# The product with w1 in seven products of quarters for the groups of 256 tokens, and transposed attention weights in two parts a pair

## The chip, the cores and the metric

The kernel runs on one core of one Trainium2 chip. The metric is the device time of a launch in microseconds: 1701.26 us before, the median of three runs (1700.86 to 1701.98). The core has TensorE for products (with a separate count of its weight loads), VectorE (DVE), ScalarE (ACT) and GpSimd (POOL) for elementwise work, and SyncE, which issues transfers.

## The reference

Attention over 8 batches of 8 heads, 576 tokens and 64 values a head, in which only the scores within tau of their row's maximum count; then, per batch, a Fourier mix of the [576, 512] result and a feed-forward pair of products. All is fp32.

```python
scores = scale * q @ k^T                          # [8, 8, 576, 576]
scores = where(scores >= max(scores) - tau, scores, -1e9)
attn   = softmax(scores) @ v                      # -> x [8, 576, 512]
u  = x + real(fft(fft(x, axis=1), axis=2))
un = (u - mean(u)) / sqrt(var(u) + 1e-6)
out = u + maximum(un @ w_ch1, 0) @ w_ch2          # w_ch1 [512, 2048], w_ch2 [2048, 512]
```

## The kernel before

The mean is taken out of w1 once and the variance's factor is applied at the end, so that the feed-forward part works on u, held transposed as u_t in a ring of two batches (1152 tokens). The first 512 tokens go in two groups by plain products; the other 4096 go in 16 groups of 256. For those the second product (with w2) is already done in seven products of quarters by Winograd's form of Strassen's method: both operands are cut into 2 x 2 quarters, sums of quarters are formed, and seven quarter products replace eight. Groups alternate between two orders ("up" and "down"), so that each leaves the sums of the weights as the next one needs them.

Everything TensorE does stands in an order fixed by the program. In each attention step i the scores of one block of 128 queries are made, `softmax` runs on VectorE and ScalarE, and the weights of the step before are transposed (`weights_in_parts`). Between these come three slots, `fill()`, in which the Fourier mix and the feed-forward groups advance by one piece or more: each `yield` ends a piece. From the third batch on, only TensorE's order is fixed; the order on the other engines is a scheduler's. All products share four PSUM banks (tag "mm"), except the scores.

The transposed weights, kept for a pair of heads, and the product with v:

```python
    def weights_in_parts(i):

        n, t = divmod(i, NT)
        e, rec = steps.pop(i)
        if t == 0:


            e_t = sb.tile([128, 8, S], FP32, tag="e_t", bufs=1, name="e_t")
            ends = sb.tile([128, S], FP32, tag="ends", bufs=1, name="ends")
            recs = None
            if rec is not None:
                recs = sb.tile([128, S], FP32, tag="sums", bufs=1, name="recs")
            vt = heads[n][2]
            # ... (v with its columns reversed, for odd pairs)
            heads[n] = (*heads[n][0:2], vt, e_t, ends, recs)
        e_t, ends, recs = heads[n][3:6]
        pe = ps.tile([128, 4, 128], FP32, tag="mm", bufs=4, name="pe")
        nc.tensor.transpose(pe[:, 0, :], e[:, 512:640], ident[:, :])
        kept = [ends]
        if rec is not None:
            nc.tensor.transpose(pe[:, 1, :], rec[:, :], ident[:, :])
            kept.append(recs)
        # ... copies of pe into ends (and recs) by ScalarE; qs: the columns of block t
        for j in range(2 if t < 4 else 1):
            pw = ps.tile([128, 4, 128], FP32, tag="mm", bufs=4, name="pw")
            if j == 1:
                yield
            for c in range(4):
                c0 = (S + D) * j + 128 * c
                nc.tensor.transpose(pw[:, c, :], e[:, c0 : c0 + 128], ident[:, :])
            if t < 4:
                nc.scalar.copy(e_t[:, 4 * j : 4 * j + 4, qs], pw[:, :, :])
            # ... the last block has both heads in one copy

    def weighted_values(n):

        b, p = n // NPAIR, PAIRS[n % NPAIR]
        _, _, vt, e_t, ends, recs = heads.pop(n)
        if n % NPAIR == 0:
            xs[b] = [None] * NPAIR
        x = sb.tile([128, S], FP32, tag=f"x{p}", bufs=1, name=f"x{p}")
        for h in range(2):
            cols = slice(HALF * h, HALF * (h + 1))
            pv = ps.tile([128, 512], FP32, tag="mm", bufs=4, name="pv")
            for c in range(5):
                for j in range(2):
                    nc.tensor.matmul(
                        pv[64 * j : 64 * j + 64, 0:HALF], vt[:, 2 * c + j, :],
                        e_t[:, 4 * j + c, cols] if c < 4 else ends[:, cols],
                        start=(c == 0), stop=(c == 4), skip_group_check=True,
                    )
            if normalized(n):
                nc.scalar.copy(x[:, cols], pv[:, 0:HALF])
            else:
                nc.vector.tensor_tensor(
                    out=x[:, cols], in0=pv[:, 0:HALF], in1=recs[:, cols], op=ALU.mult
                )
        # ... two rows swapped by transfers, for odd pairs
        xs[b][p] = x
```

The rows of a group, the product with w1, and a group of 256 tokens:

```python
    class Rows:


        def __init__(self, g):
            # ... first token, number of 128-row tiles, buffers
        def load(self):
            t = len(self.us)
            c0 = (self.first + 128 * t) % RING
            pn = ps.tile([128, 512], FP32, tag="mm", bufs=4, name="pn")
            for c in range(ND):
                nc.tensor.transpose(
                    pn[:, 128 * c : 128 * (c + 1)], u_t[:, c, c0 : c0 + 128], ident[:, :]
                )
            u = sb.tile([128, DM], FP32, tag="u", bufs=3, name="u")
            for c in (0, 256):
                nc.scalar.copy(u[:, c : c + 129], pn[:, c : c + 129])
                nc.scalar.copy(u[:, c + 129 : c + 256], _reversed(pn[:, c + 129 : c + 256]))
            # ... mean and variance of the row (VectorE)
            self.us.append(u)

        # ... factors(): rstd = 1 / sqrt(var + eps) of the loaded rows (ScalarE, VectorE)
        def add(self, t, cols, product):

            u = self.us[t][:, cols]
            nc.vector.scalar_tensor_tensor(
                out=u, in0=product, scalar=self.rstd[:, t : t + 1], in1=u,
                op0=ALU.mult, op1=ALU.add,
            )

        # ... store(t): the tile of u goes out

    def hidden(g, count, j, ht):

        # ... n tokens from column c0 of the ring; two parts where they straddle its end
        for a, z, at in parts:
            for c in range(ND):
                nc.tensor.matmul(
                    ph[:, a:z], w1[c][:, 128 * j : 128 * (j + 1)], u_t[:, c, at : at + z - a],
                    start=(c == 0), stop=(c == ND - 1), skip_group_check=len(parts) > 1,
                )
        if count % 2 == 0:
            nc.scalar.activation(out=ht, in_=ph[:, 0:n], func=ACT.Relu)
        else:
            nc.vector.tensor_relu(ht, ph[:, 0:n])

    # ... channels(g): the first two groups, by plain products

    def channels_in_quarters(g):
        if g == FIRST:
            first_sums()
        up = (g - FIRST) % 2 == 0
        rows = Rows(g)
        h = [hs[:, BT * j : BT * (j + 1)] for j in range(NJ)]
        a = [
            [[h[NK * k + p][:, 128 * i : 128 * (i + 1)] for p in range(NK)] for k in range(2)]
            for i in range(2)
        ]
        s_tile = sb.tile([128, NK, 128], FP32, tag="sums", bufs=1, name="s_tile")
        s_sum = [s_tile[:, p, :] for p in range(NK)]
        pool = nc.gpsimd

        for count in range(NJ):
            p, k = divmod(count, 2)
            hidden(g, count, NK * k + p, h[NK * k + p])
            if k == 1:

                pool.tensor_tensor(out=s_sum[p], in0=a[1][0][p], in1=a[1][1][p], op=ALU.add)
                if not up:
                    pool.tensor_tensor(out=s_sum[p], in0=s_sum[p], in1=a[0][0][p], op=ALU.subtract)
                pool.tensor_tensor(
                    out=a[1][0][p], in0=a[0][0][p], in1=a[1][0][p], op=ALU.subtract
                )
            yield 4 * ND * BT
            if count in (3, 7):
                rows.load()
                yield ND * 128
            if count == 11:
                rows.factors()

        def product(bank, left, right, start):
            for p in range(NK):
                nc.tensor.matmul(
                    bank[:, 0 : DM // 2], left[p], right[p],
                    start=start and p == 0, stop=p == NK - 1, skip_group_check=True,
                )
                if p % 2 == 1 and p < NK - 1:
                    yield 4 * DM

        # alone(): such a product in a bank of its own, then rows.add() by VectorE
        # ... fifth or seventh; product 1 opens the bank sum_; 2 alone; product 6 adds into sum_, two rows.add();
        # 3 alone; product 4 adds into sum_, rows.add(); seventh or fifth; the sums between them on GpSimd
        # (s_sum, a[0][1]) and VectorE (t_sum)
```

The slots, and the last six batches:

```python
    def fill():
        nonlocal budget, spent
        budget += per_slot
        if mixes:
            mix(1)
        while work and spent < budget and work[0][0] < mixed:
            done = next(work[0][1], None)
            if done is None:
                work.pop(0)
            else:
                spent += done

    # ... the first two batches, every engine's order fixed

    # ...
    for i in range(2 * per_batch, total + 1):
        if i < total:
            scores(i)
            softmax(i)

        n, t = divmod(i, NT)
        nothing = iter(())
        prep = prep_in_parts(n + 1) if t == 3 and n + 1 < B * NPAIR else nothing
        weights = weights_in_parts(i - 1)
        next(prep, None)
        fill()
        next(weights, None)
        fill()
        next(weights, None)
        next(prep, None)
        fill()
        next(prep, None)
        if t == 0:
            weighted_values(n - 1)
            for _ in fold_rows(n - 1):
                pass
            if n + 1 < B * NPAIR:
                load_v(n + 1)
        if i % per_batch == 0:
            start_batch(i // per_batch - 1)
    per_slot = cost(0) / 40
    while mixes or work:
        fill()
```

Of the kernel before, what the change touches and what calls it, by code (L numbers as in the profile page):

```python
# [47 lines left out]
def kernel(  # L48
# [12 lines left out]
    nc = tc.nc  # L61
# [213 lines left out]

    shift = const.tile([128, 1], FP32, name="shift")
# [231 lines left out]
    def weights_in_parts(i):  # L508
# [3 lines left out]
        if t == 0:  # L512


            e_t = sb.tile([128, 8, S], FP32, tag="e_t", bufs=1, name="e_t")
            ends = sb.tile([128, S], FP32, tag="ends", bufs=1, name="ends")
            recs = None
            if rec is not None:
                recs = sb.tile([128, S], FP32, tag="sums", bufs=1, name="recs")
            vt = heads[n][2]  # L520
            if PAIRS[n % NPAIR] % 2:
# [11 lines left out]
        e_t, ends, recs = heads[n][3:6]  # L533
        pe = ps.tile([128, 4, 128], FP32, tag="mm", bufs=4, name="pe")
# [5 lines left out]
        for c, dst in enumerate(kept):  # L540
            if t < 4:
                nc.scalar.copy(dst[:, 128 * t : 128 * t + 128], pe[:, c, :])
            else:
                for j in range(2):
                    hp = slice(64 * j, 64 * j + 64)
                    nc.scalar.copy(dst[hp, 512:S], pe[hp, c, hp])
        qs = slice(128 * t, min(128 * t + 128, S))
# [15 lines left out]
    def weighted_values(n):  # L563

        b, p = n // NPAIR, PAIRS[n % NPAIR]
        _, _, vt, e_t, ends, recs = heads.pop(n)
        if n % NPAIR == 0:
            xs[b] = [None] * NPAIR
        x = sb.tile([128, S], FP32, tag=f"x{p}", bufs=1, name=f"x{p}")
        for h in range(2):  # L570
            cols = slice(HALF * h, HALF * (h + 1))
            pv = ps.tile([128, 512], FP32, tag="mm", bufs=4, name="pv")
            for c in range(5):
                for j in range(2):
                    nc.tensor.matmul(  # L575
                        pv[64 * j : 64 * j + 64, 0:HALF], vt[:, 2 * c + j, :],
                        e_t[:, 4 * j + c, cols] if c < 4 else ends[:, cols],
                        start=(c == 0), stop=(c == 4), skip_group_check=True,
                    )
            if normalized(n):  # L580
                nc.scalar.copy(x[:, cols], pv[:, 0:HALF])  # L581
            else:
                nc.vector.tensor_tensor(
                    out=x[:, cols], in0=pv[:, 0:HALF], in1=recs[:, cols], op=ALU.mult
                )
# [254 lines left out]

# [400 lines left out]
```

## Time and profile before

| what | value |
|---|---|
| median of three runs | 1701.26 us |
| profiled execution | 1704.2 us from first to last instruction |
| mean TensorE clock granted | 0.995 of full speed |
| hidden product, line 805 | 2560 matmul records, 543.1 us busy |
| quarter products with w2, line 899 | 1792 records in three rows, 426.2 us busy |
| product with v, line 575 | 1280 records |
| transposes of the weights, line 554 | 1152 records, 168.9 us busy |

An instruction of TensorE has two records in the profile where it is an fp32 product, and one where it is a transpose. The busy time of a row is the time covered by its records together; as matmuls overlap in the pipeline, the mean of one record is longer than the distance between two. Where a rate is wanted, the distance from start to start in a timeline is the thing to read. A row of the profile names the line, the engine, the operation, what it writes and reads, the shape and the count; then busy us and the mean ns of one; then the idle time of its engine just before it, and what ended that idle time. GpSimd's spans are rough.

### The profile page before, as it was taken

To read this page: it belongs to the slowest core of one execution; us is meant where nothing else is said; L and a number is where in the kernel's file an instruction comes from. 1 tells how busy PE (TensorE), PEld (TensorE's weight loads), DVE (VectorE), ACT (ScalarE), POOL (GpSimd) and SP (SyncE) were. 2 spreads that over 40 slices of the span, in tenths; PEclk is the share of its full clock that TensorE was granted. 3 is DMA by queue.
4 is the path that set the end of the run, shared out by engine and by line. 5 is a ranking of instruction groups with operands and counts; after the bars stand their busy time and mean duration, and the time that the engine had idled before them with its cause. 6 is when DMAs were issued, how large, how long until landed. Compare 5 with 4: busy or idle time off the path is not lost.

```text
span 1704.2 us, 26612 instructions
## 1 busy us (share of the span) xinstructions
PE 1659.1 (97%) x9558; PEld 1266.5 (74%) x9558; DVE 1051.0 (62%) x2593; ACT 689.7 (40%) x1620; POOL 604.3 (35%) x1075
## 2 busy tenths in 40 slices
PE   8988989999999999999999999999999999999998
PEld 4555555576787787778878777777777788788887
DVE  6886885665566666656545766666565766543233
ACT  5764765343444343434333434343434444311100
POOL 5664563031312442243331233314341424242333
PEclk9999999999999999999999999999999999999999
DMA  5323222100010101000010010101011010000000
GB/s 163 110 53 108 71 71 55 30 19 21 22 34 22 30 6 41 22 27 22 13 28 27 22 33 11 34 22 28 21 29 34 15 35 2 13 1 13 13 13 13
DMA packets 130377, 57.34 MB, mean 34 GB/s; under 512 B 121123, under 2 KB 121125, under 8 KB 130246
## 3 DMA queue, kind: packets, MB, share of 16 engines
q1 hardware_dynamic: 128854, 55.35, 12.0%
q8 instruction: 76, 1.25, 0.3%
q14 instruction: 55, 0.45, 0.1%
q10 hardware_dynamic: 1392, 0.30, 0.1%
HBM read 46.02 MB, written 9.44 MB: 33 GB/s over the span
## 4 chain that ended last, share of the span: by engine, by line
PE 87%; DVE 5%; ACT 5%; DMA 1%; issue 1%; SPq 0%; POOL 0%; ACTq 0%; DVEq 0%; POOLq 0%
PE ph L805 28%; PE po L899 23%; PE pv L575 9%; PE sc L431 8%; PE pw L554 6%; PE po L829 3%; PE sc L442 2%; ACT e L467 2%; DVE e L475 2%; PE py L674 1%; PE pa L691 1%; DVE neg L459 1%; PE pa L695 1%; PE pe L535 1%; PE pn L765 1%; PE pq L396 1%
## 5 line engine op out<-in xcount | busy, mean ns | idle before, releaser
L805 PE MATMUL ph<-u_t,w 128*128 128x256 f32 (+2 forms) x2560 | 543.1, 362 | 5.8 <-ACT y_e L684 4.1
L805 PEld LDWEIGHTS ph<-u_t,w 128*128 128x128 f32 x2560 | 428.6, 191 | 75.4 <-issue 12.0
L459 DVE TENSOR_REDUCE neg<-sc 128x1 f32<-128x576 f32 x288 | 205.9, 751 | 217.3 <-PE sc L431 202.2
L467 ACT ACTIVATE e<-sc,neg 128x576 f32<-128x576 f32 x288 | 211.5, 734 | 309.8 <-DVE neg L459 309.6
L884 POOL TENSOR_TENSOR s_tile<-hs 128x128 f32<-128x128 f32 x128 | 62.1, 485 | 638.0 <-DVE hs L812 536.4
L475 DVE SCALAR_TENSOR_TENSOR e<-sc,thr,e 128x576 f32<-128x576 f32 x288 | 227.2, 814 | 61.1 <-ACT thr L471 60.0
L899 PE MATMUL po<-w,hs 128*128 128x256 f32 x1024 | 242.8, 382 | 0.0
L899 PEld LDWEIGHTS po<-w,hs 128*128 128x128 f32 x1024 | 187.3, 190 | 29.6 <-issue 7.0
L556 ACT COPY e_t<-pw 128x512 f32<-128x512 f32 x256 | 148.3, 593 | 119.5 <-PE pw L554 119.0
L554 PE MATMUL pw<-ident,e 128*128 128x128 f32 x1152 | 168.9, 273 | 11.1 <-ACT kT L404 4.8
L431 PE MATMUL sc<-kT,qT 64*128 64x288 f32 x1024 | 165.9, 430 | 7.8 <-DVE e L475 7.3
L554 PEld LDWEIGHTS pw<-ident,e 128*128 128x128 f32 x1152 | 135.8, 141 | 34.8 <-ACT kT L404 5.6
L812 DVE TENSOR_SCALAR hs<-ph 128x256 f32<-128x256 f32 (+2 forms) x144 | 60.5, 420 | 149.1 <-PE ph L805 134.6
L431 PEld LDWEIGHTS sc<-kT,qT 64*128 64x128 f32 x1024 | 92.0, 186 | 68.4 <-issue 43.1
L810 ACT ACTIVATE hs<-ph 128x256 f32<-128x256 f32 (+2 forms) x144 | 55.1, 383 | 214.7 <-PE ph L805 206.4
L787 DVE SCALAR_TENSOR_TENSOR u<-po,rstd,u 128x256 f32<-128x256 f32 (+1 forms) x164 | 76.1, 482 | 84.1 <-PE po L899 84.0
L491 DVE TENSOR_SCALAR e<-e,den 128x576 f32<-128x576 f32 x216 | 123.5, 608 | 3.0
L899 PE MATMUL po<-hs,s_tile 128*128 128x256 f32 x512 | 122.4, 383 | 0.0
L899 PEld LDWEIGHTS po<-hs,s_tile 128*128 128x128 f32 x512 | 93.9, 190 | 16.2 <-issue 3.0
L857 POOL TENSOR_TENSOR hs<-hs,s_tile 128x128 f32<-128x128 f32 x128 | 60.4, 490 | 83.2 <-PE po L899 82.7
L857 POOL TENSOR_TENSOR s_tile<-s_tile,hs 128x128 f32<-128x128 f32 x128 | 70.7, 579 | 28.2 <-PE po L899 28.2
L581 ACT COPY x<-pv 128x288 f32<-128x288 f32 x48 | 19.2, 399 | 147.9 <-PE pv L575 142.7
(169 smaller groups left out, 2208.3 us busy)
## 6 DMA issues: line engine op xcount, KB each, us to landing
hs<-in_moe_w_ch_dram SPq DMA_DIRECT2D x23, 512.0 KB, 4.2
out_dram<-u SPq DMA_DIRECT2D x36, 256.0 KB, 2.2
qk_in<-in_q_dram SPq DMA_DIRECT2D x64, 128.0 KB, 2.3
v_in<-in_v_dram SPq DMA_DIRECT2D x64, 128.0 KB, 2.4
qk_in<-in_k_dram SPq DMA_DIRECT2D x31, 128.0 KB, 2.5
w<-in_moe_w_ch_dram SPq DMA_DIRECT2D x6, 512.0 KB, 7.8
qk_in<-in_k_dram SPq DMA_DIRECT2D x31, 64.0 KB, 2.3
stage<-in_moe_w_ch_dram SPq DMA_DIRECT2D x3, 512.0 KB, 4.3
```

Source lines behind the costliest of these rows:

```text
L431: nc.tensor.matmul(sc[j][:, c, 0:HALF], qT[hp, 128 * t : 128 * t + 128], kT[hp, HALF * c : HALF * (c + 1)], start=True, stop=True,)
L459: nc.vector.tensor_reduce(out=neg[:, j : j + 1], in_=sc[j][:, :, 0:HALF], axis=AXIS_XY, op=ALU.max, negate=True,)
L467: nc.scalar.activation(out=ej, in_=sc[j][:, :, 0:HALF], func=ACT.Exp, bias=neg[:, j : j + 1], scale=1.0)
L475: nc.vector.scalar_tensor_tensor(out=ej, in0=sc[j][:, :, 0:HALF], scalar=thr[:, j : j + 1], in1=ej, op0=ALU.is_ge, op1=ALU.mult, accum_out ...
L491: nc.vector.tensor_scalar(out=e[:, S * j : S * (j + 1)], in0=e[:, S * j : S * (j + 1)], scalar1=den[:, j : j + 1], scalar2=None, op0=ALU.mult,
L554: nc.tensor.transpose(pw[:, c, :], e[:, c0 : c0 + 128], ident[:, :])
L556: nc.scalar.copy(e_t[:, 4 * j : 4 * j + 4, qs], pw[:, :, :])
L575: nc.tensor.matmul(pv[64 * j : 64 * j + 64, 0:HALF], vt[:, 2 * c + j, :], e_t[:, 4 * j + c, cols] if c < 4 else ends[:, cols], start=(c == ...
L787: nc.vector.scalar_tensor_tensor(out=u, in0=product, scalar=self.rstd[:, t : t + 1], in1=u, op0=ALU.mult, op1=ALU.add,)
L805: nc.tensor.matmul(ph[:, a:z], w1[c][:, 128 * j : 128 * (j + 1)], u_t[:, c, at : at + z - a], start=(c == 0), stop=(c == ND - 1), skip_gro ...
L857: eng.tensor_tensor(out=out_[p], in0=in0[p], in1=in1[p], op=op)
L899: nc.tensor.matmul(bank[:, 0 : DM // 2], left[p], right[p], start=start and p == 0, stop=p == NK - 1, skip_group_check=True,)
```

## The change

Three things change.

The product with w1 of the 16 groups of 256 tokens is done in seven products of quarters too. Left quarters are those of w1 (256 inputs x 1024 hidden channels), right quarters those of u_t (256 inputs x 128 tokens). Each of the seven products comes in two parts of 512 hidden channels, 8 calls of 128 columns in one bank. The sum that products 1, 6 and 7 share stays in one bank from the first to the last of them; the other sums are formed as the banks are read: VectorE adds, ScalarE copies and takes the relu in place. Sums of weights are kept in s_w1 and renewed in place on GpSimd and VectorE, sums of tokens in t_u on VectorE.

To make room, the transposed weights of a pair are kept for 256 and then 320 queries, in shorter tiles, and the product with v is done in two parts of these widths, the first within the pair. The rows u have two buffers, not three.

The sums for the product with w2 are formed in pieces of 512 columns on GpSimd, after the hidden product; the order of the w2 products starts with the one that needs no sum. At the start of a batch the pieces of the Fourier mix are dealt out as 3, then 0, 2, 2, 2, 2 and 4 to a slot, where there was one to a slot.

```diff
+    s_w1 = const.tile([128, 2, HID // 2], FP32, name="s_w1")
+    t_u = const.tile([128, 3, 2, 128], FP32, name="t_u")
# ... weights_in_parts: tiles of 320 columns, for blocks 0, 1 and then 2, 3, 4
-        if t == 0:
-            e_t = sb.tile([128, 8, S], FP32, tag="e_t", bufs=1, name="e_t")
-            ends = sb.tile([128, S], FP32, tag="ends", bufs=1, name="ends")
+        if t in (0, 2):
+            e_t = sb.tile([128, 8, S - 256], FP32, tag="e_t", bufs=1, name="e_t")
+            ends = sb.tile([128, S - 256], FP32, tag="ends", bufs=1, name="ends")
# ... weighted_values
-    def weighted_values(n):
+    def weighted_values(n, part):
+        m = (256, S - 256)[part]
+        cols = slice(256 * part, 256 * part + m)
+        pv = ps.tile([128, 512], FP32, tag="mm", bufs=4, name="pv")
# ... the products and copies over m columns, as before over 288; rows are loaded by number, into two buffers
-            u = sb.tile([128, DM], FP32, tag="u", bufs=3, name="u")
+            u = sb.tile([128, DM], FP32, tag="u", bufs=2, name="u")
# ... channels(1) ends with first_sums_w1(): four sums of 1024 columns on VectorE
+    HH = HID // 2
+    a_w1 = [[[w1[2 * k + c][:, HH * i : HH * (i + 1)] for c in range(2)] for k in range(2)]
+            for i in range(2)]
+    s_u = [s_w1[:, c, :] for c in range(2)]
+    def hidden_in_quarters(g, rows, quarter):
+        c0 = tokens_of(g)[0] % RING
+        c1 = (c0 + 128) % RING
+        up = (g - FIRST) % 2 == 0
+        b = [[[u_t[:, 2 * k + c, z : z + 128] for c in range(2)] for z in (c0, c1)]
+             for k in range(2)]
+        t1, t2, minus_t4 = ([t_u[:, m, c, :] for c in range(2)] for m in range(3))
+        def sums(out_, in0, in1):
+            for c in range(2):
+                nc.vector.tensor_tensor(out=out_[c], in0=in0[c], in1=in1[c], op=ALU.subtract)
+        sums(t1, b[0][1], b[0][0])
+        sums(t2, b[1][1], t1)
+        sums(minus_t4, b[1][0], t2)
+        def weights(eng, part, in0, in1, op=ALU.subtract):
+            cols = slice(512 * part, 512 * part + 512)
+            for c in range(2):
+                eng.tensor_tensor(
+                    out=s_u[c][:, cols], in0=in0[c][:, cols], in1=in1[c][:, cols], op=op
+                )
+        OPERANDS = {
+            1: (a_w1[0][0], b[0][0]), 2: (a_w1[0][1], b[1][0]), 3: (s_u, b[1][1]),
+            4: (a_w1[1][1], minus_t4), 5: (s_u, t1), 6: (s_u, t2), 7: (a_w1[1][0], b[0][1]),
+        }
+        banks = {}
+        def product(m, part):
+            name = "sum" if m in (1, 6, 7) else m
+            if m not in (6, 7):
+                banks[name] = ps.tile([128, 512], FP32, tag="mm", bufs=4, name="ph")
+            left, right = OPERANDS[m]
+            for q in range(4):
+                for c in range(2):
+                    nc.tensor.matmul(
+                        banks[name][:, 128 * q : 128 * q + 128],
+                        left[c][:, 512 * part + 128 * q : 512 * part + 128 * q + 128], right[c],
+                        start=q == 0 and c == 0 and m not in (6, 7), stop=c == 1,
+                        skip_group_check=True,
+                    )
+            return banks[name][:, :]
+        def add(to, bank, other=None):
+            nc.vector.tensor_tensor(
+                out=to, in0=bank, in1=to if other is None else other, op=ALU.add
+            )
+        def relu(to):
+            nc.scalar.activation(out=to, in_=to, func=ACT.Relu)
+        def fifth(part):
+            y = product(5, part)
+            h01, h11 = quarter(1, 0, part), quarter(1, 1, part)
+            if up:
+                nc.scalar.copy(h11, y)
+                weights(nc.gpsimd, part, s_u, a_w1[0][0])
+            else:
+                add(h01, y)
+                relu(h01)
+                add(h11, y)
+                relu(h11)
+        def third(part):
+            y = product(3, part)
+            h01 = quarter(1, 0, part)
+            if up:
+                add(h01, y)
+                relu(h01)
+            else:
+                nc.scalar.copy(h01, y)
+                weights(nc.gpsimd, part, a_w1[1][1], a_w1[1][0])
+        def first_two(part):
+            h00 = quarter(0, 0, part)
+            nc.scalar.copy(h00, product(1, part))
+            yield 4096
+            add(h00, product(2, part))
+            relu(h00)
+            yield 4096
+        def others(part):
+            h10, h01, h11 = quarter(0, 1, part), quarter(1, 0, part), quarter(1, 1, part)
+            x = product(6, part)
+            add(h01, x, h11 if up else None)
+            if up:
+                weights(nc.vector, part, a_w1[0][1], s_u)
+            else:
+                weights(nc.vector, part, s_u, a_w1[0][0], ALU.add)
+            yield 4096
+            nc.scalar.copy(h10, product(4, part))
+            yield 4096
+            x = product(7, part)
+            add(h10, x)
+            relu(h10)
+            if up:
+                add(h11, x)
+                relu(h11)
+            else:
+                nc.scalar.copy(h11, x)
+            yield 4096
+        begin, end = (fifth, third) if up else (third, fifth)
+        begin(0)
+        yield 4096
+        yield from first_two(0)
+        rows.load(1)
+        sums(b[0][1], b[1][1], b[0][1])
+        yield ND * 128
+        yield from others(0)
+        begin(1)
+        yield 4096
+        rows.load(0)
+        yield ND * 128
+        yield from first_two(1)
+        end(0)
+        yield 4096
+        rows.factors(0, 2)
+        yield from others(1)
+        end(1)
+        yield 4096
# ... channels_in_quarters: after the hidden product, the sums for w2 on GpSimd, 512 columns each
+        def s_form(out_, in0, in1, op):
+            for part in range(2):
+                place = [
+                    s_tile[:, 512 * part : 512 * part + 512] if at is None else quarter(*at, part)
+                    for at in (out_, in0, in1)
+                ]
+                nc.gpsimd.tensor_tensor(out=place[0], in0=place[1], in1=place[2], op=op)
# ... the first of the w2 products is now the one of unsummed quarters; then fifth or seventh
         if up:
-            combine(pool, s_sum, s_sum, a[0][0], ALU.subtract)
+            s_form(None, (1, 0), (1, 1), ALU.add)
+            s_form((1, 0), (0, 0), (1, 0), ALU.subtract)
+        else:
+            s_form(None, (1, 0), (1, 1), ALU.add)
+            s_form((1, 0), (0, 0), (1, 0), ALU.subtract)
+            s_form(None, None, (0, 0), ALU.subtract)
         sum_ = bank()
         yield from product(sum_, a[0][0], b00, True)
-            mix(1)
+            mix(next(pace, 1))
# ... weighted_values(n, 0) after the weights of block 1, weighted_values(n - 1, 1) after those of block 4
+            if i < total:
+                mix(3)
+                pace = iter((0, 2, 2, 2, 2, 4))
```

## The prediction

> **What bounds the kernel now.** I read the first line of the page first: which engine is busy nearly all the time.
>
> ```profile
> PE 1659.1 (97%) x9558; PEld 1266.5 (74%) x9558; DVE 1051.0 (62%) x2593; ACT 689.7 (40%) x1620; POOL 604.3 (35%) x1075
> ```
>
> TensorE leaves 45 us of 1704 unused, and no other engine is over two thirds busy. A share of the whole span hides stages, so next the busy time of each engine in three stretches: the first two batches of attention, the six batches in which attention and feed-forward work alternate, and the end, where no attention is left.
>
> ```profile
> 0.00:370.00 370.00, 339.81 (x1788) 202.98 (x1790) 269.54 (x634) 214.42 (x494) 174.88 (x254) 0.98 0.27 78
> 370.00:1480.00 1110.00, 1099.43 (x6688) 873.29 (x6685) 700.88 (x1781) 446.79 (x1040) 351.15 (x669) 1.00 0.09 24
> 1480.00:1704.00 224.00, 219.88 (x1088) 190.28 (x1086) 80.59 (x179) 28.50 (x88) 78.28 (x154) 1.00 0.03 10
> ```
>
> The columns are the stretch, its length, then busy time of TensorE, its weight loads, VectorE, ScalarE and GpSimd. In the middle TensorE lacks 10.6 us of 1110, so that stretch is TensorE work end to end; 30 of the 45 us lie in the first stretch, which holds no group of 256 tokens. Whatever TensorE work is removed from those groups is therefore removed from the time, unless TensorE then waits. What it waits for today is in the list of waits, TensorE alone:
>
> ```profile
> PE sc L431 <- DVE e L475: 7.3, 15, 1.6
> PE pw L554 <- ACT kT L404: 4.8, 3, 1.9
> PE ph L805 <- ACT y_e L684: 4.1, 4, 1.0
> ```
>
> Columns: who waited for whom, total us, times, longest. The first is score banks that VectorE has not yet emptied; the second and third are the four shared product banks (tag "mm") not yet copied out by ScalarE. These are the two places where the change can give time back. In the chain of what ended last, the hidden product (line 805) has 28% of the span and the quarter products with w2 (line 899) 23%.
>
> [...] The trace records two matmuls per fp32 product (128 for the 64 calls of a group)[...].
> [...] the normalization of e (line 491) takes 520 ns in the median and up to 1715.
>
> **Part 1: the hidden product, seven for eight.** Before, a group does 16 hidden blocks of 4 products, 256 columns each: 64 calls, 128 records. After, seven products in two parts of 8 calls: 112 calls, 224 records of 128 columns. The timeline of TensorE near the end gives the first price:
>
> ```profile
> 1647.03 7.07 PE L805 MATMUL ph<-u_t,w 128*128 128x256 f32 x32
> 1653.94 0.60 PE L765 MATMUL pn<-ident,u_t 128*128 128x128 f32 x4
> 1661.72 13.98 PE L805 MATMUL ph<-u_t,w 128*128 128x256 f32 x64
> 1675.54 3.62 PE L899 MATMUL po<-hs 128*128 128x256 f32 x16
> ```
>
> Columns: start, us, engine, line. From start to the next start, 32 records take 6.91 us and 64 take 13.82: 216 ns each. The second price is in the same kernel: where a group straddles the end of the ring of 1152 tokens, its products are split into 128 columns.
>
> ```profile
> 1383.14 1.95 PE L805 MATMUL ph<-u_t,w 128*128 128x128 f32 x16
> 1384.93 0.27 PE L535 MATMUL pe<-ident,e 128*128 128x128 f32 x1
> ...
> 1396.51 1.95 PE L805 MATMUL ph<-u_t,w 128*128 128x128 f32 x16
> 1398.39 1.24 PE L431 MATMUL sc<-kT,qT 64*128 64x288 f32 x8
> ```
>
> The first 16 records take 1.79 us to the next start: 112 ns. (The last row ends with an extra 0.09 us of switching.) Before: 14 groups x 128 x 216 ns = 387 us, and 2 straddling groups x 256 x 112 ns = 57 us, together 444. After: 16 x 224 x 112 ns = 401. **Saved: 43 us of TensorE**, 2.5%. An eighth of 444 would be 56; the 128-column form returns part of it.
>
> **Part 2: the sums around it.** Prices per row, at 512 elements:
>
> ```profile
> L375 DVE TENSOR_TENSOR w<-pr,mean 128x512 f32<-128x512 f32 x8 | 5.2, 680 | 3.2 <-PE pr L369 3.1
> ```
>
> ```profile
> L556 ACT COPY e_t<-pw 128x512 f32<-128x512 f32 x256 | 148.3, 593 | 119.5 <-PE pw L554 119.0
> L812 DVE TENSOR_SCALAR hs<-ph 128x256 f32<-128x256 f32 x128 | 53.9, 421 | 145.0 <-PE ph L805 130.7 <-PE pt L407 11.1 <-PE pe L535 3.0
> L304 ACT ACTIVATE w<-w 128x512 f32<-128x512 int32 x32 | 20.3, 633 | 23.8 <-DVE w L296 23.7
> L317 POOL TENSOR_TENSOR w<-w,hs 128x512 f32<-128x512 f32 x23 | 29.3, 1274 | 37.4 <-DVE w L312 24.6 <-ACT e L467 7.7 <-ACT thr L471 4.0
> ```
>
> Per group VectorE loses 8 relus (8 x 0.42 = 3.4 us) and gains 10 adds out of the banks, 4 sums of weights (14 x 0.68 = 9.5) and 8 small token sums (8 x 0.29 = 2.3, by the 300 ns of the 143-wide row on line 611): +8.5 us, x16 = 136, and about 5 once for the first weight sums. VectorE goes to about 1190 us, 71% of the new span. ScalarE loses 8 x 0.38 and gains 6 or 8 copies (7 x 0.59) and 8 relus (8 x 0.63): 4.2 + 5.1 - 3.1 = +6.2, x16 = 99, to 790 us. GpSimd before did 32 or 40 pieces of 128 (0.49 us each, 17.6 us a group on average); after, 12 or 14 pieces of 512 at 1.28, 16.6: the same. None of it is on TensorE, and none of these engines becomes the bound by its sum.
>
> **Part 3: transposed weights and product with v in two parts.** The same ten pairs of products, over 256 and 320 columns for 288 twice: no TensorE work saved or added. It frees about 9 KB a partition for the new weight sum and makes room by shorter tiles; u goes from three buffers to two. I count 0.
>
> **Part 4: what TensorE may newly wait for.** One bank is held from product 1 to product 7 of each part, so three "mm" banks remain for everything else during most of the hidden product. Product 7 adds into that bank, and may start only when VectorE has read product 6 from it; between lies product 4, 16 records x 112 = 1.8 us, sometimes with transposes. Without attention that is enough (0.68 us and the wait for the semaphore). With it, VectorE may be inside a softmax row (two reductions of 0.75, two 0.81, two 0.52). I put this, with the banks, at 0.8 us a group over 13 groups: 10 us, chosen, not measured. Mixing now comes in bursts of two and four pieces instead of one per slot; its last piece of each batch waits for one tmp tile that four GpSimd additions of 0.8 us release. Today mixing costs some 2.3 us in a batch; I allow 3 more in some batches: 5 us. **Sum: 1701 - 43 + 15 = 1673**; as the waits may also be filled by attention work that stands between, I take 1671.
>
> **The rivals.** (a) All of it arrives: TensorE stays gapless as it does in the middle stretch today, although a bank is already held long in the w2 products and VectorE empties all of those. Then 1701 - 43 = 1658. For it: 10.6 us of waits in 1110 today. (b) Order on VectorE becomes the bound in the middle stretch: it is at 63% there and gets some 8.5 us for each of 13 groups, 75% of the shorter stretch, in order, with longer GpSimd pieces in its way (1.28 us for 0.46). If two waits of 1 us arise per part, four a group, 50 us come back: about 1705. Against it: products and sums are spread over several slots. (c) The two-part attention and the bursts of mixing cost or save on their own in the first 370 us, where TensorE is not the bound: 5 us either way.
>
> **Range and chances.** 43 us is firm within 2 us, as both prices come from this trace. The waits are not: 0 to 40 us. That gives 1656 to 1696 for 8 in 10. The limit for 2% is 1667.2, so new waits of less than 9 us; I give that 0.4, and a loss over 34 us net 0.05.
>
> **What would show it.** TensorE's hidden rows should be 3584 records of 128 columns, 112 ns from start to start in the last stretch; its busy time should fall by about 43 us, to about 1616; VectorE should be near 1190. In the list of waits, new rows of ph on VectorE's additions into hs are Part 4; rows of pw or pa on ScalarE are the banks. The prediction is wrong if the records come slower than 112 ns (weights written by VectorE and GpSimd just before they are loaded), or if the waits in the middle stretch exceed 45 us.

## The result: 45 us less on TensorE, and none of it in the time

The changed kernel takes 1707.05 us in the median of four runs (1705.85 to 1708.69), beside 1701.62 us of the kernel before in the same comparison: ratio 1.0032, 95% interval 1.0015 to 1.005. 1671 was predicted, 1656 at the lowest and 1696 at the highest. The profiled executions of the two kernels, 1704.1 and 1704.2 us, differ by less than the medians; the comparison of traces below accounts for the absence of the gain, not for the last 5 us.

First the busy times of the whole span, on the page of the changed kernel:

```profile
PE 1631.2 (96%) x10838; PEld 1283.4 (75%) x10838; DVE 1224.0 (72%) x2822; ACT 775.4 (46%) x1735; POOL 616.4 (36%) x707
```

TensorE is busy 28 us less and the span is the same, so TensorE stands idle 28 us longer: 1704.1 - 1631.2 = 73 us against 45. Where, the same three stretches tell:

```profile
0.00:370.00 370.00, 335.49 (x1756) 197.12 (x1757) 268.00 (x637) 215.85 (x490) 172.85 (x252) 0.99 0.28 78
370.00:1480.00 1110.00, 1082.88 (x7663) 890.31 (x7662) 835.95 (x1959) 510.54 (x1132) 367.71 (x394) 1.00 0.09 24
1480.00:1704.00 224.00, 212.83 (x1425) 195.95 (x1423) 120.05 (x229) 48.98 (x115) 75.82 (x62) 0.98 0.03 10
```

Idle time of TensorE by stretch (length less first busy time): 34.5, 27.1 and 11.2 us, where the kernel before had 30.2, 10.6 and 4.1. The middle stretch, nearly gapless before, has lost 16 us, the end 7 and the start 4.

The price of the hidden product is as predicted. TensorE's timeline at the end of the changed kernel, where no attention is left (line 917 is the new product's matmul):

```profile
1655.28 1.95 PE L917 MATMUL ph<-t_u,s_w 128*128 128x128 f32 x16
1657.07 1.95 PE L917 MATMUL ph<-t_u,w 128*128 128x128 f32 x16
```

From 1655.28 to 1657.07, 16 records take 1.79 us: 112 ns each (the mean of one record there is 275 ns, as they overlap). The whole account, from the traces: time from the start of one matmul to the start of the next, without idle time, added up by the tile that is written.

| TensorE, us | before | after | difference |
|---|---|---|---|
| hidden product (ph, all groups) | 514.5 | 469.5 | -45.0 |
| product with v (pv) | 164.2 | 169.9 | +5.7 |
| product with w2 (po) | 453.6 | 458.4 | +4.8 |
| transposes of the weights (pw) | 132.6 | 135.8 | +3.2 |
| all other tiles | | | +3 |
| idle between matmuls | 39.2 | 67.0 | +27.8 |

Together the rows below the first return the 45. What TensorE waits for in the changed kernel, beside the list shown for before:

```profile
PE pw L559 <- DVE qT L400: 7.0, 3, 2.3
PE pv L582 <- ACT e_t L563: 6.6, 3, 3.0
PE pv L582 <- ACT tmp L715: 6.4, 5, 1.4
PE ph L917 <- DVE hs L926: 6.1, 4, 4.3
PE sc L434 <- DVE e L478: 6.0, 15, 1.2
...
PE po L1058 <- DVE qT L400: 2.9, 1, 2.9
PE po L1058 <- DVE u L795: 2.2, 1, 2.2
```

The second and fifth belong to attention and nearly all lie in the first 300 us. New are the other five rows, few and long waits: on VectorE's copy of q (line 400, two rows), on ScalarE's copy into tmp (line 715), on VectorE's addition of a product's bank (line 926), and on its addition of a w2 product to u (line 795). In time they stand together, where a batch's Fourier transform, the mix, begins (about 320, 530, 710 to 735, 960, 1145, 1330 us) and in the tail after 1480. Between, in the ordinary groups, TensorE waits for its sum bank under 4 us in all.

At the fourth of these places the timeline shows how such a wait is made. GpSimd and VectorE rows, and the one TensorE row that waits (in brackets: idle time before the row, and what ended it):

```profile
957.84 1.48 POOL L726 TENSOR_TENSOR u_t<-x,tmp 128x287 f32<-128x287 f32 x2
957.91 0.86 DVE L891 TENSOR_TENSOR t_u<-u_t 128x128 f32<-128x128 f32 x1 [0.42 <-POOL u_t L722]
...
964.78 0.87 DVE L891 TENSOR_TENSOR t_u<-u_t,t_u 128x128 f32<-128x128 f32 x1 [1.87 <-POOL u_t L722]
...
966.22 0.77 DVE L891 TENSOR_TENSOR t_u<-u_t,t_u 128x128 f32<-128x128 f32 x1 [0.58 <-POOL u_t L722]
...
968.25 0.74 DVE L400 TENSOR_SCALAR qT<-pq,q_scale 128x512 f32<-128x512 f32 x1
969.04 0.66 PE L559 MATMUL pw<-ident,e 128*128 128x128 f32 x4 [2.33 <-DVE qT L400]
```

Line 891 is the sums of tokens that the new product needs. They read u_t, which GpSimd is still making (lines 722 and 726). At 964.81 TensorE has finished what the copy of q (line 400) reads. But the sums stand ahead of the copy in VectorE's queue, and VectorE runs its queue in order here: it finishes one sum, stands idle 0.58 us for GpSimd, makes the next, then two maxima of the softmax, and starts the copy at 968.25. TensorE needs the bank that the copy empties: 2.33 us of waiting.

In the tail it is another queue. VectorE and TensorE in the changed kernel:

```profile
1499.45 1.86 DVE L645 TENSOR_TENSOR f<-f 128x608 f32<-128x608 f32 x1
1501.23 1.53 DVE L669 SCALAR_TENSOR_TENSOR f<-sums,factors 128x304 f32<-128x304 f32 x1
...
1503.07 0.97 DVE L669 SCALAR_TENSOR_TENSOR f<-f,factors 128x304 f32<-128x304 f32 x2
...
1504.34 0.68 DVE L926 TENSOR_TENSOR hs<-ph,hs 128x512 f32<-128x512 f32 x1
1505.08 3.78 PE L917 MATMUL ph<-u_t,w 128*128 128x128 f32 x16 [4.33 <-DVE hs L926]
```

Product 7 waits 4.33 us for line 926, the addition that reads product 6 out of the sum bank; ahead of it VectorE does the combinations with which the last batch's mix begins. And the 16 records after the wait take 3.57 us to the next start, not 1.79. The granted clock is the figure after the five busy times in these two short stretches of the same kernel:

```profile
1501.00:1505.00 4.00, 0.00 (x0) 0.00 (x0) 4.00 (x8) 0.37 (x1) 1.43 (x1) 0.83 0.00 0
1505.00:1508.40 3.40, 3.32 (x15) 3.32 (x16) 0.62 (x2) 0.00 (x0) 0.00 (x0) 0.50 0.00 0
```

The half clock lasts until 1510.5, over 5.4 us of work from 1505.08 on, and half of that, 2.7 us, is lost. So this wait of 4.3 us cost seven. Up to the last microsecond, every stretch of half clock in the two traces lasts 3.4 or 6.8 us, at a granted clock of 0.50, and a wait of 2.17 us, at 1537.73 in the changed kernel, was followed by one too (the last section has the count). Before had four of them, 17 us in all; after has seven, 31 us, which is up to 7 us of the growth in the other rows (3.9 us in po, 0.9 in pw, 0.8 in pv).

### The profile page after: what moved, and what is told of

Its sections match the earlier page's. It is cut to its first block, busy times and chain, and to the rows that moved or that the text cites. A ratio compares the mean times of both kernels' runs of the same rounds, so it can differ in the third digit from the quotient of the medians.

```text
span 1704.1 us, 29009 instructions
## 1 busy us (share of the span) xinstructions
PE 1631.2 (96%) x10838; PEld 1283.4 (75%) x10838; DVE 1224.0 (72%) x2822; ACT 775.4 (46%) x1735; POOL 616.4 (36%) x707
## 3 DMA queue, kind: packets, MB, share of 16 engines
q8 instruction: 86, 1.41, 0.3%
## 4 chain that ended last, share of the span: by engine, by line
PE 76%; DVE 12%; ACT 7%; POOL 3%; issue 2%; DVEq 0%; ACTq 0%; POOLq 0%
PE po L1058 22%; PE ph L917 21%; PE pv L582 8%; PE sc L434 7%; PE pw L559 6%; PE po L839 3%; DVE e L478 2%; DVE neg L462 2%; ACT e L470 2%; PE sc L445 2%; POOL u_t L722 1%; PE ph L813 1%; PE py L683 1%; POOL u_t L726 1%; PE pd L112 1%
## 5 line engine op out<-in xcount | busy, mean ns | idle before, releaser
L917 PE MATMUL ph<-u_t,w 128*128 128x128 f32 x1536 | 189.7, 279 | 6.7 <-DVE hs L926 4.8
L917 PEld LDWEIGHTS ph<-u_t,w 128*128 128x128 f32 x1536 | 180.5, 194 | 10.3 <-DVE hs L926 5.1
L926 DVE TENSOR_TENSOR hs<-ph,hs 128x512 f32<-128x512 f32 x160 | 107.3, 685 | 77.0 <-PE ph L917 51.3
L1054 POOL TENSOR_TENSOR s_tile<-hs 128x512 f32<-128x512 f32 x32 | 52.8, 1649 | 243.9 <-ACT hs L931 243.9
L494 DVE TENSOR_SCALAR e<-e,den 128x576 f32<-128x576 f32 x216 | 135.2, 663 | 2.6
L917 PE MATMUL ph<-t_u,s_w 128*128 128x128 f32 x1024 | 125.2, 276 | 0.0
L917 PEld LDWEIGHTS ph<-t_u,s_w 128*128 128x128 f32 x1024 | 119.1, 192 | 4.4 <-issue 2.3
L900 POOL TENSOR_TENSOR s_w<-s_w,w 128x512 f32<-128x512 f32 x32 | 40.9, 1300 | 223.1 <-PE ph L917 211.6
L931 ACT ACTIVATE hs<-hs 128x512 f32<-128x512 f32 x128 | 80.0, 632 | 86.8 <-DVE hs L926 86.4
L900 POOL TENSOR_TENSOR s_w<-w,w 128x512 f32<-128x512 f32 x32 | 40.0, 1272 | 211.5 <-PE ph L917 211.5
```

Of the source, the lines that this page charges most:

```text
L494: nc.vector.tensor_scalar(out=e[:, S * j : S * (j + 1)], in0=e[:, S * j : S * (j + 1)], scalar1=den[:, j : j + 1], scalar2=None, op0=ALU.mult,
L900: eng.tensor_tensor(out=s_u[c][:, cols], in0=in0[c][:, cols], in1=in1[c][:, cols], op=op)
L917: nc.tensor.matmul(banks[name][:, 128 * q : 128 * q + 128], left[c][:, 512 * part + 128 * q : 512 * part + 128 * q + 128], right[c], start ...
L926: nc.vector.tensor_tensor(out=to, in0=bank, in1=to if other is None else other, op=ALU.add)
```

## The experiments

Theory A at the start was that the mix in a burst is the cost. Its rivals were VectorE's order (rival b of the prediction) and the product with v in two parts. Kernel 3 gave the latter its form, theory D: the first half is copied into x half a pair of heads earlier than before, while the last batch's mix may still read the same buffer of x. Kernel 1 is the kernel of experiment 1, and so on; all ratios are to the kernel before.

**1. The burst taken out of the changed kernel (the mix one piece per slot, as before).**

```diff
         if i % per_batch == 0:
             start_batch(i // per_batch - 1)
-            if i < total:
-                mix(3)
-                pace = iter((0, 2, 2, 2, 2, 4))
```

> The changed kernel with the Fourier mix dealt out one piece to a slot, as before. Theory A (the burst of mix pieces makes TensorE wait: about 22 of the 27.8 us of new idle time lie around a batch's start): TensorE's idle time falls from 67 us to some 45, the half-clock stretches at 735 and 1155 us vanish, and the time is 1680 to 1690. Rival B (VectorE's load of additions out of the banks is the cause, the burst only where it shows): the waits move elsewhere, idle stays above 60 us, the time stays within 1700 to 1710. Rival C (the two-part product with v costs it): no change here, 1707.

Measured: 1765.02 us, ratio 1.036 (1.0341 to 1.0378). Without the burst it is 58 us slower, outside the range of all three theories, so the burst is a remedy. For what, the next experiments show. The first row in this kernel's list of waits is TensorE waiting for the addition of product 6:

```profile
PE ph L917 <- DVE hs L926: 25.2, 9, 4.8
```

**2. The burst alone, put into the kernel before.** The same three lines added, with `mix(next(pace, 1))` in `fill`.

> The kernel before with the burst of mix pieces at each batch's start as the only change. Theory A: the burst alone costs, with no quarter product of w1 and no added VectorE work: 10 to 20 us more idle time of TensorE, 1711 to 1722. Rival B: the burst is harmless while VectorE is at 62%: within 4 us of 1701.

Measured: 1704.8 us, ratio 1.0013 (1.0004 to 1.0022): 2 us, in rival B's range; theory A falls.

**3. Part 3 alone, put into the kernel before** (`weights_in_parts` and `weighted_values(n, part)` as in the diff above, nothing else).

> The kernel before with the transposed weights and the product with v in two parts as the only change. Theory C (each pair now switches twice to and from the product with v, which shows as 5.7 us more in its rows): 4 to 8 us slower, 1705 to 1709. Rival (the 5.7 us are half-clock stretches that fall on these rows): within 2 us of 1701.

Measured: 1732.93 us, ratio 1.0168 (1.0149 to 1.0188): 30 us for a part counted as 0, and far over theory C's 4 to 8. The product with v takes 6.2 us more from start to start, with the same columns in sum. TensorE goes over to it twice a pair, not once: at full clock, after the first 250 us, a pair takes 5.00 us in one visit in the kernel before, and 2.31 and 2.84 us in two visits here, as in the changed kernel, 0.15 us more, or 4.8 in 32 pairs; the rest of the 6.2 was put down to half clock. Most of what remains of the 30 are waits at the beginning of batches (9.4 us more idle time) and half clock after them (17 us more of it, 8.5 us lost; the granted clock was 0.990 over the whole execution, 0.995 in the kernel before). The kernel before where ScalarE copies a batch's first pair into x, and then this kernel at one of those places:

```profile
988.75 0.40 ACT L581 COPY x<-pv 128x288 f32<-128x288 f32 x1 [5.85 <-PE pv L575]
```

```profile
994.02 0.30 PE L537 MATMUL pe<-ident,e 128*128 128x128 f32 x1 [1.92 <-DVE den L480]
...
994.90 0.89 POOL L723 TENSOR_TENSOR u_t<-x,tmp 128x287 f32<-128x287 f32 x1
...
995.83 0.37 ACT L585 COPY x<-pv 128x256 f32<-128x256 f32 x1 [1.04 <-POOL u_t L723]
996.25 0.64 PE L697 MATMUL pa<-seq_even,y_e 128*1 128x145 f32 x2 [0.55 <-ACT x L585]
```

ScalarE's copy of the first half into x waits for GpSimd, which reads the x of the last batch in the mix, and TensorE waits for ScalarE. Before, these copies wait for TensorE, never for GpSimd; here four of them wait for GpSimd, 4.1 us in all. Theory D comes from these lines. The longer wait ahead, 1.92 us for VectorE's den, comes at four batch starts (7.7 us); these lines do not tie it to x, and only kernel 6 does, whose list has no such row.

**4. The sums of tokens on GpSimd (changed kernel).** They then stand in the queue of the engine that makes what they read, and no longer ahead of the copy of q.

```diff
-        sums(t1, b[0][1], b[0][0])
-        sums(t2, b[1][1], t1)
-        sums(minus_t4, b[1][0], t2)
+        sums(t1, b[0][1], b[0][0], nc.gpsimd)
+        sums(t2, b[1][1], t1, nc.gpsimd)
+        sums(minus_t4, b[1][0], t2, nc.gpsimd)
```

> The changed kernel with the three sums of tokens of a group (t1, t2, -t4) on GpSimd in place of VectorE. Theory A2 (these sums stand in VectorE's queue ahead of the copy of qT and wait there for the last additions of the mix, so that one product bank is held and TensorE waits 2.3 to 2.9 us at four batch starts): those four waits, 9.9 us in all, vanish, with the two half-clock stretches after them; 1690 to 1697. Rival: GpSimd delivers the sums late, TensorE waits for them at the start of the groups instead, 1700 to 1715.

Measured: 1692.54 us, ratio 0.993 (0.9914 to 0.9947): 14 us off the changed kernel, in theory A2's range. The four waits for the copy of q (9.9 us) are gone from the list, and the one for u (2.2 us) too. The edit takes the sums off VectorE as well as from ahead of the copy; a kernel that only moves them behind it was not run.

**5 and 6. A second buffer of x for the first pair of a batch,** added to kernel 1 and to kernel 3. Room came from letting two small constant tiles and rec lie in the tile of the token sums (in kernel 3 there is room).

```diff
-            xs[b][p] = sb.tile([128, S], FP32, tag=f"x{p}", bufs=1, name=f"x{p}")
+            xs[b][p] = sb.tile([128, S], FP32, tag=f"x{p}", bufs=1 + (p == PAIRS[0]), name=f"x{p}")
```

> The changed kernel with the mix one piece to a slot and with two buffers for x of the first pair of a batch (its room comes from tables that share the tile of the token sums). Theory D (the first half of the product with v of a batch's first pair now comes while the last batch's mix still reads the same single buffer of x; its copy out waits, and with it a product bank and ScalarE's queue; the burst is there to end the mix sooner): without that wait the even mix is no worse than the burst; from the 1765 of the even mix alone to 1690 to 1705. Rival B (VectorE's additions out of the banks make the even mix slow): 1740 or more.

> The kernel before with the product with v in two parts, even mix as before, and two buffers for x of a batch's first pair. Theory D: of the 30 us that the two parts alone cost, only the switching is left, 6 us, so 1706 to 1711; the repeated waits of 1.9 us for pe and for the copy of x at four batch starts vanish. Rival (the two parts cost by what they do to ScalarE and the banks everywhere): 1725 or more.

Measured: 1728.24 us (ratio 1.0143, 1.0121 to 1.0164), 37 us off kernel 1; and 1707.27 us (1.0019, 1.0012 to 1.0027), 26 us off kernel 3, so that Part 3 with a second buffer costs 3 us. Kernel 6 is where theory D put it, and in it ScalarE's copies into x wait for GpSimd no longer. So with one buffer of x, two parts need a mix that is done early: that is one use of the burst. It is not the only one: kernel 5 misses theory D's 1690 to 1705 by 23 us, and the row of 25.2 us for product 6's addition still stands in its list. Experiments 7 to 10 take that up.

**7. Kernel 5 with the sums of tokens on GpSimd (the edit of 4).**

> The changed kernel with even mix, two buffers for x of a batch's first pair, and the token sums on GpSimd. If both causes are right and add up: 10 us under the one with two buffers alone, 1675 to 1690. If the token sums block VectorE only where the mix comes in a burst: no better than that one.

Measured: 1720.04 us, ratio 1.0094 (1.0077 to 1.011); 8 us off kernel 5, where neither expectation put it. Kernel 5 had hardly a wait for the copy of q (0.8 us); what went are three waits of 1.8 us for ScalarE's copy of ends and one of 2.2 us for u. The list of waits has one row above all others, the same as in kernels 1 and 5:

```profile
PE ph L917 <- DVE hs L926: 25.2, 9, 4.8
```

This is the wait of the tail above, here at five batch starts too.

**8. The changed kernel with burst, sums on GpSimd and two buffers of x.**

> As before it, but with the mix in a burst. Theory D: with two buffers the burst has lost its use and keeps its cost, the waits of the product with v for the tmp tile (1 to 2 us at five batch starts): 1685 to 1692, a few us above the even mix. If the burst is good in itself: below the even mix.

Measured: 1692.09 us, ratio 0.993 (0.9913 to 0.9947), as kernel 4: under the burst the second buffer brings nothing. The time is at the edge of theory D's range, but not for its reason: beside kernel 7, the same with an even mix, the burst saves 28 us, so it has not lost its use.

**9. Kernel 4 with the mix's first work on VectorE in pieces.** The mix began with one lump of seven combinations and then three empty steps; the steps now stand between the pieces, and the groups' work falls between them. On the burst's own three steps this changes nothing; only the tail changes.

```diff
         fold_chunks(nc.vector, b, 0)
+        yield 0
         # ... one sum and the first of three combinations
+            if at == 0:
+                yield 0
         # ... two combinations and a difference
-        for _ in range(3):
-            yield 0
+        yield 0
```

> The kernel with the token sums on GpSimd (1692.5 us), and the fold and combination work of VectorE at the start of a mix cut by the mix's three empty steps, one piece per step, in place of one lump followed by three empty steps. In the burst nothing stands between the steps, so only the last batch changes: VectorE's add of product 6 comes ahead of four of the combinations. Theory F, the lump in VectorE's queue is what product 7 waits for: the idle of 4.3 us at 1491 falls under 1.5 us, and the 16 records after it go back from 3.5 us to 1.8, so about 1687 us. Rival G, TensorE has nothing to feed it there and the wait only moves to another instruction: 1692 us.

Measured: 1686.65 us, ratio 0.9899 (0.9882 to 0.9915): 6 us, as theory F had it. In the profiled executions 4.5 us of this lie in the tail; the rest is half clock elsewhere (over the whole execution the granted clock was 0.992 in kernel 4 and is 0.995 here). The tail again (line numbers are two higher in this kernel: 928 is the addition, 919 the product):

```profile
1488.77 1.86 DVE L645 TENSOR_TENSOR f<-f 128x608 f32<-128x608 f32 x1
1490.55 0.68 DVE L928 TENSOR_TENSOR hs<-ph,hs 128x512 f32<-128x512 f32 x1
...
1491.28 2.05 PE L919 MATMUL ph<-u_t,w 128*128 128x128 f32 x16 [1.22 <-DVE hs L928]
```

The addition comes ahead of the combinations, the wait is 1.22 us in place of 4.33, and the records run at full clock (1.00 from 1489 to 1496 us).

**10. Kernel 7 (even mix) with the same edit.**

> The kernel with even mix, two buffers of x for the first pair and token sums on GpSimd (1720.0 us), with the combinations cut by the empty steps as in e9_sums_spread; here that moves product 6's add ahead of the combinations in every batch. Theory F: the five gaps of 2.4 to 4.8 us ahead of product 7 (17 us) and part of the 47 us at half clock go, about 1720 - 17 - 10 = 1693 us. Rival G: the waits come from GpSimd's or ScalarE's pieces of the mix, which stay where they are: 1715 us or more.

Measured: 1694.39 us, ratio 0.9944 (0.9929 to 0.9959): 26 us off kernel 7, as theory F had it. So the other use of the burst was to keep this lump away from product 6's addition: with the lump cut, the even mix is within 2 us of kernel 8. The row that had 25.2 us in its list has 3.0:

```profile
PE ph L919 <- DVE hs L928: 3.0, 4, 1.2
```

**11. Kernel 8 with the same edit and a milder burst.**

```diff
-                pace = iter((0, 2, 2, 2, 2, 4))
+                pace = iter((0, 2, 2, 2, 2))
```

> The kernel with the burst, two buffers of x and token sums on GpSimd (1692.1 us), with the combinations cut as in e9_sums_spread, and the burst without its last four pieces at once: they come one by one, as the second buffer of x allows. In the kernel before this change to it, five waits of 1.0 to 2.0 us of the product with v for ScalarE's copy into tmp, together 8 us, follow the four pieces. Theory H, those waits are the price of four pieces at once: they go, and with the tail's 5 us the time is about 1679 us. Rival: the pieces wait for the same single tmp tile wherever they stand, or meet product 6 and 7 as the even mix does: 1687 us or more.

Measured: 1678.24 us, ratio 0.9848 (0.9834 to 0.9863), the fastest of all: 29 us less than the changed kernel, 25 less than the kernel before, and close to theory H's 1679. Kernel 10, with an even mix, is 16 us slower; why was not taken apart. The stretches of this kernel:

```profile
0.00:370.00 370.00, 335.66 (x1759) 197.17 (x1760) 264.65 (x633) 216.29 (x491) 176.35 (x259) 0.99 0.28 78
370.00:1480.00 1110.00, 1096.39 (x7820) 902.84 (x7819) 820.72 (x1913) 520.06 (x1156) 401.02 (x467) 1.00 0.09 24
1480.00:1676.00 196.00, 190.12 (x1263) 175.08 (x1262) 104.02 (x183) 38.81 (x89) 82.51 (x78) 1.00 0.03 12
```

The middle stretch lacks 13.6 us of 1110, after 27.1, and no stretch of half clock is left after the first 300 us: the granted clock was 0.98 in these and 0.997 over all 1676.5 us, so that by estimate from these figures under 1.4 us can be lost after them, less than the 1.7 us that a stretch of 3.4 us costs. The waits of the product with v for tmp (8 us in kernels 4 and 9) are gone, although the milder burst hands the pieces to the same single tmp tile. Kernel 11 also has the second buffer of x; a milder burst without it was not run.

## Why the prediction was wrong

**Part 1, right.** 43 us were to be saved on TensorE; 45.0 were, and a record costs 112 ns. Kernel 11 turns 25 of them into time, once most of the waits are gone. The price itself was measured, and held.

**Part 2, sums too small, conclusion right.** VectorE was put at about 1190 us and has 1224. The 128 sums of tokens were priced at 0.29 us, 37 in all, and took 56.5; the 64 sums of weights took 53.2 for 43.5, and the normalization of e 135.2 where it had 123.5. The 32 sums of tokens that write t1 have a median of 0.83 us. Beside GpSimd such a sum took three times as long: in the changed kernel 0.86 us at 957.91 beside GpSimd, 0.28 at 970.71 without. ScalarE (775 for 790) and GpSimd (616 for "the same", 604) were right. None became the bound by its sum.

**Part 3, "I count 0", failed.** Columns were counted and nothing else. Two things were missing: going to the product with v twice a pair costs TensorE 4.8 us at full clock (its rows grew by 5.7 us in the changed kernel and 6.2 in kernel 3, half clock included), and writing the first half of x earlier collides with the last batch's mix. Kernel 3 shows the sum, 30 us, and kernel 6 that all but 3 of it go with a second buffer. In the changed kernel the burst hides this: ScalarE's copies into x still wait 10.8 us for GpSimd, but no row of TensorE waits for them. So Part 3 shows there as the 5.7 us and as the price of the burst.

**Part 4, 15 us, failed in place and in size.** The 10 us for the sum bank were too many for the ordinary groups (under 4 us), and the 5 us for the mix far too few. Its three terms, each removed by an experiment:

| what TensorE waits for at the mix | removed by | us |
|---|---|---|
| copy of q behind token sums that wait for GpSimd (and u, in the tail) | kernel 4 | 14.5 |
| product 6's addition behind the first combinations (tail) | kernel 9 | 5.9 |
| the four last pieces at once | kernel 11 against 9 | 8.4 |
| sum: changed kernel to kernel 11 | | 28.8 |

The third term holds the second buffer of x as well. Each is the net of waits and of the half clock after them, and a difference of medians from comparisons in which the kernel before itself measured 1701.6 to 1704.0 us, so good to some 2 us; that they add up to the whole proves nothing, as each starts where the last one ends. So the mix's term was nearer 29 us than 5: put into the prediction's sum with 4 for the sum bank and the 6 of Part 3, it gives 1701 - 43 + 29 + 4 + 6 = 1697, still 10 short of the time; what is left lies in the waits of half a microsecond to one that remain in kernel 11 (9 us more idle time than before, the 4 among them) and in rows that grew, such as the transposes of the weights by 3 us; it was not taken apart. The step from 1673 to 1671, because attention would fill waits, found nothing behind it.

**The rivals.** (a), everything arrives: 1658; no kernel came there, and 20 us remain between it and kernel 11, of which 9 are idle and some 4 the product with v. (b), "order on VectorE becomes the bound", about 1705, has the time but not the picture: its four waits of 1 us a group did not come. VectorE's order did decide, but in a handful of places where a long queue stands ahead of a bank that TensorE needs. (c), the burst and the two parts within 5 us either way, was right on the burst alone (2 us, kernel 2) and wrong on the two parts (30 us, kernel 3), and it looked at the first 370 us, while the loss lay after them.

**The signs named.** 3584 records at 112 ns: right. Rows of ph waiting for VectorE's additions, named as Part 4's: 6.1 us, of which 4.3 are the one wait in the tail; the copy of q, 9.9 us, was not named. Busy time down by 43 us to 1616: it fell by 28 to 1631, as half clock and two visits to the product with v made other rows longer. Waits in the middle stretch over 45 us: 27, so this sign would have passed the prediction; it was set for one stretch and for waits alone, while the loss is spread over waits, clock and switching.

## What to carry to other kernels

When a product is replaced by fewer products and more sums, price the sums by where they stand in their engine's order, not by their duration: ask of each new instruction what it waits for and which bank's release stands behind it, and put it on the engine that makes its input. When a result is written in two parts, the first part is written earlier; check that the buffer is free then. Long lumps in an engine's queue can be cut with pieces of the critical product's own sums between, without any change in the work.

## What was not expected of the hardware

A wait of 2.17 us (at 1537.73 in the changed kernel) was followed by half clock, 3.41 us at 0.50, and in the wait of 4.33 us 6.83 us of it began, so that this wait cost 7. The length of a wait does not tell it alone: of three waits of 2.3 us in the changed kernel one was followed by half clock. Where the wait falls goes with it. In the trace before and in the one after, all these stretches begin on one grid of 3.413 us: those of the changed kernel at 735.68, 1155.52, 1503.68 and 1541.22 us lie 123, 102 and 11 grid steps apart. Between 330 and 1640 us and from full clock, half clock followed each of the 4 grid steps of the changed kernel in which TensorE had no matmul for 2.10 to 2.93 us, none of its 372 others, with 1.44 us at most, and none of the 383 of the kernel before, with 1.30 at most. The three waits of 2.3 us put at most 1.26, 2.20 and 1.41 us into one step, and only the second was followed. In the first 330 us the two traces do not part so cleanly: the seven steps that were followed have 1.09 to 2.81 us, the 177 others up to 1.70. The sums of 128 columns, 0.28 us alone (970.71 in the changed kernel), took 0.86 beside GpSimd (957.91).
